# Writing the output in three column groups of 256 instead of two halves of 384, with fewer loads between the stores

## The chip, the core and the metric

The kernel runs on one core of a Trainium2 chip. The metric is the device time of one execution in microseconds (us). TensorE is called PE here, VectorE DVE, ScalarE ACT, GpSimd POOL, and SyncE, which in this kernel only issues transfers (DMAs), SP.

## The reference

An attention with a sigmoid in place of the softmax feeds a soft mixture of experts: 8 batches of 448 tokens (3584 in all), 12 heads of 64 (768 columns), 8 experts with 4 slots each (32 slots), hidden width 1024, all in 32-bit floats.

```python
scores = scale * (q @ k.T) - log(S); x = sigmoid(scores) @ v         # x: 3584 x 768
logits = x @ phi                                                     # 3584 x 32
d = softmax of logits over the tokens;  slot_input = d.T @ x         # 32 x 768
h = relu(slot_input[e] @ w1[e]);  slot_out[e] = h @ w2[e]            # w1: 8 x 768 x 1024, w2: 8 x 1024 x 768
c = softmax of logits over the slots;  out = c @ slot_out            # out: 3584 x 768
```

w1 and w2 hold 25 MB each, and the output 11 MB.

## The kernel before

**Stages.** The first stage is the attention with the logits and the slot inputs; it ends near 298 us, and the change does not touch it. Then come two stages: w1 (`w1_part` and `h_part`, one expert after another), and w2 with the output, from the loop at L600 to the end.

**Weights.** They are cut on the host into 128 units of 128 x 768 floats, 384 KB each: units 0 to 63 are w1, 64 to 127 are w2. In the kernel before a w2 unit holds, for one half of the output columns (`HALF` = 384), two of the 64 pieces of 128 rows that the 8 experts have together (`NFC` = 8 per expert). Units go in order into a ring of 68 tiles (`ring_tile`: 49 called wa, 19 called wb). `load_unit` issues the next one on SP. In the attention 49 are issued, 19 after it, and the others by `load_more` in the loops over w1 and over the first half of w2, as tiles come free; `load_more` stops `N_LATE` = 16 units before the end. SP issues in program order, and a transfer that waits holds up all that come after it.

**w2.** `w2_step` does half an expert: four matmuls whose stationary operand is 128 x 32 (hT), each in its own 32 rows of the PSUM tile `po`, with the columns of the group as moving operand. So 16 steps make one half of the columns. `gather` copies `po` to SBUF on ACT, `sum_groups` adds the four row groups up with one matmul by `rep`, and DVE copies the result to `st`.

**Output.** `out_batch` does one batch of 448 tokens for one half of the columns: four matmuls (128, 128, 96 and 96 tokens), then two evictions into ring tiles, one by ACT (2 x 128 tokens) and one by DVE (2 x 96 tokens), and two stores that are put in a list. Each store writes pieces of one row's columns: 256 and 192 pieces per batch. `store(n)` issues the first n in the list on SP.

**Order.** The first half's outputs are written while the second half's steps run: in step i = 3 + b stands `out_batch` of batch b. In the first `N_MIX` = 4 of these, SP gets two stores and then four of the late units. `warm(3)` puts three small matmuls on PE that only keep it busy. After the last step SP gets what is left in the list (batches 4 to 7 of the first half), then the second half's eight batches follow.

Of the kernel before, what the change touches and what calls it, by code (L numbers as in the profile page):

```python
# [9 lines left out]
F32 = mybir.dt.float32  # L10
# [6 lines left out]
B, H, S, D = 8, 12, 448, 64  # L17
DM, NSLOT, E, SPE, F = 768, 32, 8, 4, 1024
P = 128
# [3 lines left out]
NQ = NPR // 2  # L23
NKC = DM // P
NFC = F // P
HALF = DM // 2
UNIT = 768
N_A = 49
N_B = 19
N_LATE = 16  # L30
N_MIX = 4
NATT = 5
QW = 2 * S
NP = B * NPR
# [6 lines left out]
TOK = (128, 128, 96, 96)  # L41
# [6 lines left out]
def soft_moe_attention(ctx: ExitStack, tc: tile.TileContext, qk, v, phi, w1, w2, cst, out):  # L48
    nc = tc.nc
# [7 lines left out]
    ident = csb[:, 0:128]  # L57
    rep = csb[:, 128:256]
# [4 lines left out]
    lt_all = cpool.tile([P, B, P], F32, name="lt_all")  # L63
# [6 lines left out]
    nc.gpsimd.memset(lt_all, NEG)  # L70

    units = [("w1", e, 2 * uu + y, kh) for e in range(E) for uu in range(2) for kh in range(2) for y in range(2)]
    units += [("w2", hf, e, g, y) for hf in range(2) for e in range(E) for g in range(2) for y in range(2)]
    state = {"next": 0, "ring": 0, "wpb": None}
    utile = {}

    def ring_tile(dt=F32):
        n = state["ring"]
        state["ring"] = n + 1
        n %= N_A + N_B  # L80
        if n < N_A:
            return wpa.tile([P, UNIT], dt, name=f"wa{n}")
        return state["wpb"].tile([P, UNIT], dt, name=f"wb{n - N_A}")

    def load_unit():
        n = state["next"]
        if n >= len(units):
            return
        state["next"] = n + 1
        u = units[n]  # L90
        t = ring_tile()[:]
        nc.sync.dma_start(t, w1[u[1:]] if u[0] == "w1" else w2[u[1:]])
        utile[u] = t
# [22 lines left out]
    with ExitStack() as actx:  # L116
# [216 lines left out]
        def last_job(b, lg):  # L333
# [15 lines left out]
            nc.scalar.activation(pe, lg, AF.Exp, bias=cw[:, 0:1])  # L349
            nc.scalar.activation(cw[:, 1:2], mz[:, 0:1], AF.Exp, bias=cw[:, 0:1])  # L350
            warm(2)
            nc.tensor.matmul(pa[0:1, 0, 0:P], m1[:, 1:2], ident, start=True, stop=True)
            warm(2)
            widen(b, pe)
            mrow = small.tile([1, 1, NSLOT], F32, name="mrow")
# [3 lines left out]
            for j in range(4):  # L359
                nc.tensor.matmul(pa[32 * j:32 * j + 32, 1, 0:1], mrow[:, 0, :], csb[0:1, 0:1], start=True, stop=True)  # L360
            warm(1)
            sl = slot_mm(b, (2, 3))
            nc.vector.tensor_tensor(out=cw[:, 2:3], in0=m1[:, 1:2], in1=pa[:, 1, 0:1], op=ALU.subtract)
# [123 lines left out]
    sb2 = ctx.enter_context(tc.tile_pool(name="sb2", bufs=1, reuse_waits="tile"))  # L487
    hT = []
# [11 lines left out]
    ps_o = ctx.enter_context(tc.tile_pool(name="ps_o", bufs=2, space=PSUM, reuse_waits="tile"))  # L500

    def px_tile():
        return ps_x.tile([P, 2, 512], F32, name="px")

    def load_more():
        if state["next"] < len(units) - N_LATE:
            load_unit()

    for _ in range(N_B):
# [2 lines left out]
    def w1_part(e):  # L512
        ph = px_tile()
        for uu in range(2):
            for k2 in range(NKC // 2):
                for j in range(4):
                    kh, kc = divmod(2 * k2 + j % 2, 3)
                    nc.tensor.matmul(  # L518
                        ph[32 * j:32 * j + 32, uu, 0:256], sT[:, 3 * kh + kc, :],
                        utile[("w1", e, 2 * uu + j // 2, kh)][:, kc * 256:(kc + 1) * 256],  # L520
                        start=(k2 == 0), stop=(k2 == NKC // 2 - 1))
                if k2 > 0:
                    load_more()
                    load_more()
            if e == 0 and uu == 0:
                finish(ps_x)
        return ph
# [26 lines left out]
            combine_d(B - 1, sb2.tile([P, P], F32, name="tmp")[:])  # L554
    h_part(*prev)

    def out_batch(hf, b, st):
        pf = [px_tile() for _ in range(2)]
        for j in range(4):
            r = slice(32 * j, 32 * j + 32)  # L560
            nc.tensor.matmul(  # L561
                pf[j // 2][0:TOK[j], j % 2, 0:HALF], lt_all[r, b, 0:TOK[j]], st[r, :], start=True, stop=True)
        for g in range(2):
            n = TOK[2 * g]
            ov = ring_tile()[0:n, :].rearrange("p (j c) -> p j c", j=2)
            (nc.scalar.copy if g == 0 else nc.vector.tensor_copy)(ov, pf[g][0:n, :, 0:HALF])  # L566
            r0 = b * S + TOF[2 * g]
            stores.append((out[r0:r0 + 2 * n, hf * HALF:(hf + 1) * HALF].rearrange("(j p) c -> p j c", p=n), ov))

    stores = deque()  # L570

    def store(n):
        for _ in range(min(n, len(stores))):
            nc.sync.dma_start(*stores.popleft())

    def warm(n):
        for _ in range(n):
            nc.tensor.matmul(wt[:, 0:P], ident, ident, start=True, stop=True)

    def w2_step(po, hf, e, g):  # L580
        for fl in range(4):
            ut = utile[("w2", hf, e, g, fl // 2)][:, fl % 2 * HALF:(fl % 2 + 1) * HALF]
            nc.tensor.matmul(  # L583
                po[32 * fl:32 * fl + 32, 0:HALF], hT[e][:, 4 * g + fl, :], ut,
                start=(e == 0 and g == 0), stop=(e == E - 1 and g == 1))

    def gather(po):
        so = sb2.tile([P, HALF], F32, name="tmp")
        nc.scalar.copy(so[:], po[:, 0:HALF])
        return so  # L590

    def sum_groups(so):
        pr = px_tile()[:, 0, :]
        nc.tensor.matmul(pr[:, 0:HALF], rep, so[:], start=True, stop=True)
        st = sb2.tile([P, HALF], F32, name="st", bufs=2)
        nc.vector.tensor_copy(st[:], pr[:, 0:HALF])  # L596
        return st

    po = ps_o.tile([P, 512], F32, name="po")
    for e in range(E):  # L600
        for g in range(2):
            w2_step(po, 0, e, g)
            load_more()
            load_more()
    so = gather(po)
    po = ps_o.tile([P, 512], F32, name="po")
    wt = ps_o.tile([P, 512], F32, name="po")
    for i in range(2 * E):
        w2_step(po, 1, *divmod(i, 2))
        if i == 1:  # L610
            st = sum_groups(so)
        if 3 <= i < 3 + B:
            out_batch(0, i - 3, st)
            if i < 3 + N_MIX:
                store(2)
                for _ in range(N_LATE // N_MIX):
                    load_unit()
        if 2 + B <= i < 2 * E - 2:
            warm(3)
    so = gather(po)  # L620
    store(len(stores))
    st = sum_groups(so)
    for b in range(B):
        out_batch(1, b, st)
        store(2)


# [33 lines left out]
```

## Time and profile before

| what | value |
|---|---|
| time, median of 3 runs | 397.97 us (396.63 to 399.82) |
| time of the profiled execution | 401.23 us |
| its span on the core | 399.5 us |
| mean granted PE clock | 0.98 |
| busy: PE, DVE, ACT | 93%, 57%, 47% |
| read from HBM, written to it | 85.43 MB, 11.47 MB |
| transfers of weights | 128 of 384 KB |
| transfers of output | 16 of 384 KB, 16 of 288 KB |

Times inside the execution are counted from the span's start. Two things lie beside the span: the 1.7 us between it and the execution's time, and the difference between this execution and the median of the runs, which is 3.3 us lower. A busy PE is not a PE at its limit, since the ends of its matmuls are modelled; and a DMA share of 1.0 or a little more means that all 16 engines move data all the time.

### The profile page before, as it was taken

Reading aid. Unit: us, or ns where it says so; the run is one execution under the profiler, and the core shown is the slowest. Engines: PE = TensorE matmul, PEld = TensorE weight load, DVE = VectorE, ACT = ScalarE, POOL = GpSimd, SP = SyncE. Lnnn points to the kernel's source line nnn. Section 1 sums busy time; section 2 is a strip of 40 time slices with the busy share of each in tenths; the row PEclk is TensorE's granted clock in tenths of the full one; section 3 lists DMA queues with packets and bytes.
Section 4 is the critical chain, followed back from the end, with each engine's and each line's share of the span. In section 5 each row is a group of like instructions: output and inputs, shape, how many; then the busy total and the mean of one; then the engine's idle time right before and its main releaser. Section 6 shows DMA issues by size and latency. Waiting matters only on the chain.

```text
span 399.5 us, 9562 instructions
## 1 busy us (share of the span) xinstructions
PE 371.3 (93%) x4000; PEld 195.1 (49%) x4000; DVE 228.7 (57%) x531; ACT 186.1 (47%) x244; POOL 3.4 (1%) x13
## 2 busy tenths in 40 slices
PE   8999999999999999899999999999989989978740
PEld 6555455555545555365545556555465543223210
DVE  3566668668777766765677777677532420330340
ACT  5655666662566656265625666564530110220330
POOL 1000000000000000000000000000010000000000
PEclk9999999999999999989999999999999999999985
DMA  7556567645655755475546656632899999999996
GB/s 237 197 189 232 180 235 257 222 150 161 225 199 192 276 199 178 140 250 178 180 120 251 220 175 239 235 126 71 304 344 334 405 400 400 400 410 409 355 288 205
DMA packets 41851, 97.52 MB, mean 244 GB/s; under 512 B 4304, under 2 KB 16208, under 8 KB 41808
## 3 DMA queue, kind: packets, MB, share of 16 engines
q1 hardware_dynamic: 41808, 96.91, 69.1%
q8 instruction: 31, 0.51, 0.5%
q14 instruction: 12, 0.10, 0.1%
HBM read 85.43 MB, written 11.47 MB: 243 GB/s over the span
## 4 chain that ended last, share of the span: by engine, by line
PE 78%; DMA 12%; DVE 3%; issue 2%; SPq 1%; ACT 0%; ACTq 0%
PE b L186 25%; PE b L168 21%; PE b L195 6%; PE px L518 5%; PE b L307 4%; PE po L583 4%; PE b L179 4%; DMA wb<-in_w_dram 4%; DMA zd<-t 3%; PE b L215 3%; PE px L561 2%; DMA dr<-zd 2%; DMA wa<-in_w_dram 2%; DMA out_dram<-wa 1%; PE px L535 1%
## 5 line engine op out<-in xcount | busy, mean ns | idle before, releaser
L158 ACT ACTIVATE att<-b,nbias 128x896 f32<-128x896 f32 x144 | 132.1, 1020 | 1.3 <-PE b L168 1.1
L186 PE MATMUL b<-att,v 128*64 128x448 f32 x576 | 115.3, 545 | 0.1
L168 PE MATMUL b<-qs,ks 64*128 64x448 f32 x864 | 96.3, 373 | 0.7 <-issue 0.5
L168 PEld LDWEIGHTS b<-qs,ks 64*128 64x128 f32 x864 | 80.2, 188 | 24.8 <-PE b L195 14.8
L186 PEld LDWEIGHTS b<-att,v 128*64 128x64 f32 x576 | 38.5, 137 | 62.6 <-issue 47.4
L158 ACT ACTIVATE attm<-b,nbias 128x896 f32<-128x896 f32 x24 | 24.2, 1010 | 71.6 <-PE b L179 71.6
L147 DVE CAST qs<-qkt 128x448 fp32r<-128x448 f32 x48 | 18.8, 392 | 51.5 <-DMA qkt<-in_qk_dram 47.4
L149 DVE TENSOR_TENSOR qs<-qkt,qs 128x448 fp32r<-128x448 f32 x48 | 30.0, 626 | 1.6
L204 DVE COPY xT<-b 128x896 f32<-128x896 f32 x23 | 25.1, 1090 | 8.6 <-PE b L195 8.5
L149 DVE TENSOR_TENSOR ks<-qkt,ks 128x384 fp32r<-128x384 f32 x48 | 26.8, 558 | 1.6
L210 DVE STREAM_TRANSPOSE y<-xT 128x448 f32<-128x448 f32 x48 | 27.3, 618 | 0.4
L179 PE MATMUL b<-qkt 64*64 64x448 f32 x192 | 22.9, 538 | 2.2 <-issue 2.2
L195 PE MATMUL b<-attm,v 64*64 64x448 f32 x192 | 23.6, 562 | 0.0
L307 PE MATMUL b<-y,dr 32*32 32x192 f32 x896 | 20.0, 332 | 0.8 <-DMA dr<-zd 0.5
L566 DVE COPY wa<-px 96x768 f32<-96x768 f32 x13 | 12.2, 952 | 13.5 <-PE px L561 12.7
L518 PE MATMUL px<-wa,sT 128*32 128x256 f32 x294 | 17.8, 381 | 0.9 <-DVE sT L378 0.9
L566 ACT COPY wa<-px 128x768 f32<-128x768 f32 x13 | 10.3, 799 | 17.9 <-PE px L561 15.2
L561 PE MATMUL px<-st,lt_all 32*128 32x384 f32 (+1 forms) x128 | 16.7, 525 | 1.5 <-DVE st L596 0.7
L215 PEld LDWEIGHTS b<-xT,phit 128*32 128x32 f32 x384 | 9.1, 109 | 17.0 <-issue 11.3
L147 DVE CAST ks<-qkt 128x384 fp32r<-128x384 f32 x47 | 16.6, 353 | 0.0
L215 PE MATMUL b<-xT,phit 128*32 128x96 f32 (+1 forms) x384 | 16.0, 266 | 0.2
L307 PEld LDWEIGHTS b<-y,dr 32*32 32x32 f32 x896 | 12.8, 103 | 6.5 <-DMA dr<-zd 2.3
(132 smaller groups left out, 223.4 us busy)
## 6 DMA issues: line engine op xcount, KB each, us to landing
wa<-in_w_dram SPq DMA_DIRECT2D x96, 384.0 KB, 7.7
qkt<-in_qk_dram SPq DMA_DIRECT2D x48, 448.0 KB, 5.0
wb<-in_w_dram SPq DMA_DIRECT2D x32, 384.0 KB, 7.1
v<-in_v_dram SPq DMA_DIRECT2D x24, 448.0 KB, 3.3
out_dram<-wa SPq DMA_DIRECT2D x13, 384.0 KB, 5.8
out_dram<-wa SPq DMA_DIRECT2D x13, 288.0 KB, 5.6
dr<-zd SPq DMA_DIRECT2D x28, 64.0 KB, 2.0
out_dram<-wb SPq DMA_DIRECT2D x3, 384.0 KB, 7.3
```

What stands on the lines that cost most here:

```text
L147: copy(dst[:, 0, :], src)
L149: nc.vector.tensor_tensor(out=dst[:, 1, :], in0=src, in1=dst[:, 0, :].bitcast(F32), op=ALU.subtract)
L158: nc.scalar.activation(att[:], sc[:, :, 0:S], AF.Sigmoid, bias=nbias, scale=QSCALE)
L168: nc.tensor.matmul(sc[:, h, 0:S], ks[r, z, c * P:(c + 1) * P], qs[r, y, :], start=(z + y == 0), stop=(z == 1))
L179: nc.tensor.matmul(sc[r, h, 0:S], t[d, S + NQK:QW], t[d, 0:S], start=True, stop=True)
L186: nc.tensor.matmul(avs["p", p][r, 0:S], vs[n][:, i * (NFULL + 1) + c, r], atts[p, c][:, h, :], start=(start and c == 0), stop=(stop and c ...
L195: nc.tensor.matmul(avs["p", 2 * n + i][d, 0:S], vt[r, NFULL, d], att[r, h, :], start=start, stop=stop)
L204: nc.vector.tensor_copy(xTs[n][:], avs[n][:, :, 0:S])
L210: nc.vector.transpose(ys[b][:, hp, :], xTs["p", p])
L215: nc.tensor.matmul(lp[32 * j:32 * j + 32, 0:TOK[j]], phi_sb[:, p % NPR, :], xTs["p", p][:, TOF[j]:TOF[j] + TOK[j]], start=(first and m == ...
L307: nc.tensor.matmul(sl[a // 2][32 * j:32 * j + 32, a % 2, 0:NPR * BLK], drs[b][32 * a:32 * a + 32, j, c * BLK:(c + 1) * BLK], y[32 * a:32 * ...
L518: nc.tensor.matmul(ph[32 * j:32 * j + 32, uu, 0:256], sT[:, 3 * kh + kc, :], utile[("w1", e, 2 * uu + j // 2, kh)][:, kc * 256:(kc + 1) * ...
```

## The change

Columns are written in three groups of 256 (`CG`). The host cuts w2 anew: a unit now holds three pieces of 128 x 256, so a group takes 21 1/3 units, and a step 1 1/3. There are 24 batches of output in place of 16, each with pieces of 1024 B in place of 1536 B (stores of 256 KB and 192 KB). The groups are called 0, 1 and 2 here. All but 18 units are issued ahead. Between the stores of group 0 stand eight of those 18, one after each batch; between the stores of group 1 stand ten, two after each of its first five batches. `warm` is gone.

```diff
-HALF = DM // 2
+NCG = 3
+CG = DM // NCG
-N_LATE = 16
-N_MIX = 4
+LATE = ((1,) * B, (2,) * 5)
...
-    units += [("w2", hf, e, g, y) for hf in range(2) for e in range(E) for g in range(2) for y in range(2)]
+    units += [("w2", i) for i in range(NCG * E * NFC // 3)]
...
     def load_more():
-        if state["next"] < len(units) - N_LATE:
+        if state["next"] < len(units) - sum(LATE[0] + LATE[1]):
...
-    def warm(n):
-        for _ in range(n):
-            nc.tensor.matmul(wt[:, 0:P], ident, ident, start=True, stop=True)
...
-    def w2_step(po, hf, e, g):
+    def w2_step(po, cg, e, g):
         for fl in range(4):
-            ut = utile[("w2", hf, e, g, fl // 2)][:, fl % 2 * HALF:(fl % 2 + 1) * HALF]
+            u, y = divmod((cg * E + e) * NFC + 4 * g + fl, 3)
             nc.tensor.matmul(
-                po[32 * fl:32 * fl + 32, 0:HALF], hT[e][:, 4 * g + fl, :], ut,
+                po[32 * fl:32 * fl + 32, 0:CG], hT[e][:, 4 * g + fl, :], utile["w2", u][:, y * CG:(y + 1) * CG],
                 start=(e == 0 and g == 0), stop=(e == E - 1 and g == 1))
...
+    for cg in range(NCG):
+        po = ps_o.tile([P, 512], F32, name="po")
+        for i in range(2 * E):
+            w2_step(po, cg, *divmod(i, 2))
+            if cg == 0:
+                load_more()
+                load_more()
+                continue
+            if i == 1:
+                st = sum_groups(so)
+            if 3 <= i < 3 + B:
+                b = i - 3
+                out_batch(cg - 1, b, st)
+                if b < len(LATE[cg - 1]):
+                    store(2)
+                    for _ in range(LATE[cg - 1][b]):
+                        load_unit()
+        so = gather(po)
     store(len(stores))
     st = sum_groups(so)
     for b in range(B):
-        out_batch(1, b, st)
+        out_batch(NCG - 1, b, st)
         store(2)
```

On SP, before, at the end of the units issued ahead (wa and wb are ring tiles, filled from the weights by L92, or written to the output by L574):

```order
L92 DMA wa_4031<-in_w_dram 128x768
L92 DMA wa_4033<-in_w_dram 128x768
L574 DMA out_dram<-wa_4240 128x2x384
L574 DMA out_dram<-wa_4242 96x2x384
L92 DMA wa_4246<-in_w_dram 128x768
L92 DMA wa_4248<-in_w_dram 128x768
L92 DMA wa_4250<-in_w_dram 128x768
L92 DMA wb_4252<-in_w_dram 128x768
L574 DMA out_dram<-wb_4264 128x2x384
L574 DMA out_dram<-wb_4266 96x2x384
```

And now, at the same place:

```order
L92 DMA wa_4025<-in_w_dram 128x768
L574 DMA out_dram<-wa_4235 128x2x256
L574 DMA out_dram<-wa_4237 96x2x256
L92 DMA wa_4241<-in_w_dram 128x768
L574 DMA out_dram<-wa_4253 128x2x256
L574 DMA out_dram<-wa_4255 96x2x256
L92 DMA wa_4259<-in_w_dram 128x768
L574 DMA out_dram<-wa_4271 128x2x256
L574 DMA out_dram<-wb_4273 96x2x256
L92 DMA wb_4277<-in_w_dram 128x768
```

The first store has moved ahead of two units (those that were in wa_4031 and wa_4033), and one batch of stores stands ahead of every late unit here, where it was one batch ahead of four.

On SP, before, around the last unit (the rows end with the last group's first batch):

```order
L92 DMA wb_4324<-in_w_dram 128x768
L574 DMA out_dram<-wa_4336 128x2x384
L574 DMA out_dram<-wa_4338 96x2x384
L574 DMA out_dram<-wa_4350 128x2x384
L574 DMA out_dram<-wa_4352 96x2x384
L574 DMA out_dram<-wa_4364 128x2x384
L574 DMA out_dram<-wa_4366 96x2x384
L574 DMA out_dram<-wa_4378 128x2x384
L574 DMA out_dram<-wa_4380 96x2x384
L574 DMA out_dram<-wa_4434 128x2x384
L574 DMA out_dram<-wa_4436 96x2x384
```

And now:

```order
L92 DMA wa_4504<-in_w_dram 128x768
L92 DMA wa_4506<-in_w_dram 128x768
L574 DMA out_dram<-wa_4518 128x2x256
L574 DMA out_dram<-wa_4520 96x2x256
L574 DMA out_dram<-wa_4532 128x2x256
L574 DMA out_dram<-wa_4534 96x2x256
L574 DMA out_dram<-wa_4546 128x2x256
L574 DMA out_dram<-wa_4548 96x2x256
L574 DMA out_dram<-wa_4588 128x2x256
L574 DMA out_dram<-wa_4590 96x2x256
```

Between the last unit and the last group's first store stood four batches; now there are three smaller ones.

On PE, before, the end of the w2 steps (L583, in the PSUM tile po), the `warm` matmuls (L578), the sum (L594) and the first output of the last group (L561):

```order
L583 MATMUL po<-wb_4294,h_3698 32x384 x2
L583 MATMUL po<-wb_4296,h_3698 32x384 x2
L578 MATMUL po<-csb 128x128 x3
L583 MATMUL po<-wb_4298,h_3698 32x384 x2
L583 MATMUL po<-wb_4300,h_3698 32x384 x2
L578 MATMUL po<-csb 128x128 x3
L583 MATMUL po<-wb_4318,h_3699 32x384 x2
L583 MATMUL po<-wb_4320,h_3699 32x384 x2
L583 MATMUL po<-wb_4322,h_3699 32x384 x2
L583 MATMUL po<-wb_4324,h_3699 32x384 x2
L594 MATMUL px<-tmp,csb 128x384
L561 MATMUL px<-st,lt_all 128x384 x2
```

And now, from the last batch of group 1 on (L579 are the steps, L590 is the sum):

```order
L561 MATMUL px<-st,lt_all 96x256 x2
L579 MATMUL po<-wa_4446,h_3697 32x256 x2
L579 MATMUL po<-wa_4464,h_3697 32x256 x2
L579 MATMUL po<-wa_4464,h_3698 32x256
L579 MATMUL po<-wa_4466,h_3698 32x256 x3
L579 MATMUL po<-wa_4484,h_3698 32x256 x3
L579 MATMUL po<-wa_4486,h_3698 32x256
L579 MATMUL po<-wa_4486,h_3699 32x256 x2
L579 MATMUL po<-wa_4504,h_3699 32x256 x3
L579 MATMUL po<-wa_4506,h_3699 32x256 x3
L590 MATMUL px<-tmp,csb 128x256
L561 MATMUL px<-st,lt_all 128x256 x2
```

The matmuls between these steps are gone, and a unit serves three matmuls where it served two.

More of the change, by code (lines that the diff above doesn't have):

```diff
@@ L555, in soft_moe_attention, with out_batch @@
     h_part(*prev)
-    def out_batch(hf, b, st):
+    def out_batch(cg, b, st):
         pf = [px_tile() for _ in range(2)]
@@ L561, in out_batch @@
             nc.tensor.matmul(
-                pf[j // 2][0:TOK[j], j % 2, 0:HALF], lt_all[r, b, 0:TOK[j]], st[r, :], start=True, stop=True)
+                pf[j // 2][0:TOK[j], j % 2, 0:CG], lt_all[r, b, 0:TOK[j]], st[r, :], start=True, stop=True)
         for g in range(2):
             n = TOK[2 * g]
-            ov = ring_tile()[0:n, :].rearrange("p (j c) -> p j c", j=2)
-            (nc.scalar.copy if g == 0 else nc.vector.tensor_copy)(ov, pf[g][0:n, :, 0:HALF])
+            ov = ring_tile()[0:n, 0:2 * CG].rearrange("p (j c) -> p j c", j=2)
+            (nc.scalar.copy if g == 0 else nc.vector.tensor_copy)(ov, pf[g][0:n, :, 0:CG])
             r0 = b * S + TOF[2 * g]
-            stores.append((out[r0:r0 + 2 * n, hf * HALF:(hf + 1) * HALF].rearrange("(j p) c -> p j c", p=n), ov))
+            stores.append((out[r0:r0 + 2 * n, cg * CG:(cg + 1) * CG].rearrange("(j p) c -> p j c", p=n), ov))
     stores = deque()
@@ L574, in store @@
             nc.sync.dma_start(*stores.popleft())
-    def warm(n):
-        for _ in range(n):
-            nc.tensor.matmul(wt[:, 0:P], ident, ident, start=True, stop=True)
-    def w2_step(po, hf, e, g):
+    def w2_step(po, cg, e, g):
         for fl in range(4):
-            ut = utile[("w2", hf, e, g, fl // 2)][:, fl % 2 * HALF:(fl % 2 + 1) * HALF]
+            u, y = divmod((cg * E + e) * NFC + 4 * g + fl, 3)
             nc.tensor.matmul(
-                po[32 * fl:32 * fl + 32, 0:HALF], hT[e][:, 4 * g + fl, :], ut,
+                po[32 * fl:32 * fl + 32, 0:CG], hT[e][:, 4 * g + fl, :], utile["w2", u][:, y * CG:(y + 1) * CG],
                 start=(e == 0 and g == 0), stop=(e == E - 1 and g == 1))
     def gather(po):
-        so = sb2.tile([P, HALF], F32, name="tmp")
-        nc.scalar.copy(so[:], po[:, 0:HALF])
+        so = sb2.tile([P, CG], F32, name="tmp")
+        nc.scalar.copy(so[:], po[:, 0:CG])
         return so
@@ L593, in sum_groups @@
         pr = px_tile()[:, 0, :]
-        nc.tensor.matmul(pr[:, 0:HALF], rep, so[:], start=True, stop=True)
-        st = sb2.tile([P, HALF], F32, name="st", bufs=2)
-        nc.vector.tensor_copy(st[:], pr[:, 0:HALF])
-        return st
[L599 to L620, printed above, removed]
+        nc.tensor.matmul(pr[:, 0:CG], rep, so[:], start=True, stop=True)
+        st = sb2.tile([P, CG], F32, name="st", bufs=2)
+        nc.vector.tensor_copy(st[:], pr[:, 0:CG])
+        return st
+    for cg in range(NCG):
[16 more added lines that the diff above has]
+        so = gather(po)
     store(len(stores))
@@ L642 @@
     w1 = inputs["moe_w1"].reshape(E, 2, 3, P, 4, 256).transpose(0, 4, 1, 3, 2, 5).reshape(E, 4, 2, P, UNIT)
-    w2 = inputs["moe_w2"].reshape(E, 2, 2, 2, P, 2, HALF).transpose(5, 0, 1, 3, 4, 2, 6).reshape(2, E, 2, 2, P, UNIT)
+    w2 = inputs["moe_w2"].reshape(E, 2, 2, 2, P, NCG, CG).transpose(5, 0, 1, 3, 2, 4, 6).reshape(-1, 3, P, CG)
+    w2 = w2.transpose(0, 2, 1, 3).reshape(-1, P, UNIT)
     cst = np.zeros((P, CW), np.float32)
```

## The prediction

> **What bounds the kernel now.** I read the page first, then a table by stretches, then the chain that ended last, and at the end the rows of single operations. The page's 40 slices (10 us each) give the first answer.
>
> ```profile
> span 399.5 us, 9562 instructions
> DMA  7556567645655755475546656632899999999996
> GB/s 237 197 189 232 180 235 257 222 150 161 225 199 192 276 199 178 140 250 178 180 120 251 220 175 239 235 126 71 304 344 334 405 400 400 400 410 409 355 288 205
> ```
>
> PE has 93% of the span on the page, but that is an average over stages. In the last eleven slices the transfer engines are full, and in the last three they are still full while the GB/s fall from 409 to 355, 288 and 205. The table by stretches shows what else works there.
>
> ```profile
> core 0: us, PE busy (x) PEld busy (x) DVE busy (x) ACT busy (x) POOL busy (x), PEclk, DMA share, GB/s
> 330.00:344.00 14.00, 14.00 (x150) 4.91 (x142) 1.43 (x2) 1.28 (x2) 0.00 (x0) 1.00 1.03 401
> 344.00:371.00 27.00, 23.21 (x166) 7.98 (x164) 6.76 (x8) 5.59 (x7) 0.00 (x0) 1.00 1.04 407
> 371.00:375.00 4.00, 2.62 (x16) 0.93 (x16) 0.56 (x1) 0.48 (x1) 0.00 (x0) 1.00 1.07 397
> 378.00:396.00 18.00, 6.20 (x40) 2.28 (x40) 5.58 (x7) 4.12 (x6) 0.00 (x0) 0.74 0.90 280
> 396.00:399.50 3.50, 0.00 (x0) 0.00 (x0) 0.00 (x0) 0.00 (x0) 0.00 (x0) 0.50 0.24 69
> ```
>
> Loads alone (330 to 344), loads mixed with stores (344 to 371) and the first stores alone (371 to 375) all run at 397 to 407 GB/s. Then something changes: from 378 to 396 only stores are left, the engines show 0.90 busy, and they move 280 GB/s. No compute engine is busy for more than 6.2 of these 18 us. So **the end is a queue of transfers**: it starts full and ends in a slow stretch of stores. The chain names the same.
>
> ```profile
> 356.53 7.32 DMA wb<-in_w_dram
> ...
> 363.92 7.35 DMA wb<-in_w_dram
> ...
> 371.33 5.76 DMA out_dram<-wa
> ...
> 384.60 0.95 DVE wa L566
> ```
>
> The last unit lands at 363.92 + 7.35 = 371.3. The last eviction ends at 385.6, 13.9 us before the span does, so the stores alone set the end.
>
> **What the change does to the queue, up to the last weights.** The bytes stay the same; pieces of output shrink from 1536 B to 1024 B, and stores and loads change order. The price of a piece comes from the two stretches that hold one kind alone.
>
> ```profile
> DMA packets 2048, 5.61 MB, mean 401 GB/s; under 512 B 227, under 2 KB 227, under 8 KB 2047
> DMA packets 834, 1.20 MB, mean 398 GB/s; under 512 B 56, under 2 KB 834, under 8 KB 834
> ```
>
> The first row is 330 to 344: 2047 - 227 = 1820 pieces of 3072 B (the 227 are 4-byte signals), 14.0 us x 16 engines x 1.03 / 1820 = 127 ns each. The second is 371.6 to 374.6 with a share of 1.066: 834 - 56 = 778 pieces of 1536 B, 3.0 x 16 x 1.066 / 778 = 66 ns. A line through both gives 46 ns for 1024 B, which this trace has in no stretch of its own. A batch is 448 pieces, before and after: 448 x 66 / (16 x 1.066) = **1.73 us before and 1.20 after** (448 x 46). The bounds are 1.15 (the same time per byte) and 1.73 (the same time per piece); I take 1.20, as the two rows lie on one line.
>
> Ahead of the last unit in SP's order stood 112 + 16 units and 4 batches; now there are 110 + 18 units and 8 + 5 = 13 batches. The engines are full all along, so the last unit lands 13 x 1.20 - 4 x 1.73 = 8.7 us later, at **380.0** (bounds 379.3 and 386.9).
>
> This needs the queue to stay full, and the change adds waits to it: every late unit now stands on SP behind two stores that wait for an eviction, and group 2's steps wait for these units.
>
> ```profile
> 300.49 41.20 SPq L92 DMA_DIRECT2D wa<-in_w_dram  x44
> 343.90 0.90 SPq L574 DMA_DIRECT2D out_dram<-wa  x2
> 376.13 0.38 SPq L574 DMA_DIRECT2D out_dram<-wa  x1
> ```
>
> SP is through with the last unit ahead at 341.7, waits for the first eviction until 343.9, and the stretch from 344 on still moves 407 GB/s: the 7 us of transfers that are under way cover such a wait. In the change it gets to the first store two units (2 x 0.98 us, 384 KB at 401 GB/s) earlier, at 339.7. When is that store ready?
>
> ```profile
> 327.43 11.75 PE po L583 x144
> 308.90 2.80 PE L518 MATMUL px<-wa,sT 128*32 128x256 f32 x48
> 337.96 0.48 ACT L589 COPY tmp<-po 128x384 f32<-128x384 f32 x1 [9.70 <-PE po L583]
> 339.11 0.91 PE L594 MATMUL px<-tmp,csb 128*128 128x384 f32 x2
> 340.06 0.56 DVE L596 COPY st<-px 128x384 f32<-128x384 f32 x1 [12.13 <-PE px L594]
> 342.11 0.92 PE L561 MATMUL px<-st,lt_all 32*128 32x384 f32 x8
> 343.07 0.80 ACT L566 COPY wa<-px 128x768 f32<-128x768 f32 x1 [4.63 <-PE px L561]
> ```
>
> A matmul in the program is two instructions in the trace. The w2 steps start at 327.4, and 256 columns into 32 rows cost 2.80 / 48 = 58 ns (L518, the same shape). Group 0's 128 instructions end at 334.9, four steps of group 1 (32) take 1.9, and the sum, its copy, one batch and its eviction at their old prices 0.91 + 0.56 + 0.92 + 0.80 = 3.2: 340.0 at the latest, 339 with two thirds of these prices. After that PE needs 0.5 us per step and at most 0.9 per batch, against 1.20 + 0.98 = 2.2 us of transfers per batch and unit. Of the later stores, batch b of group 1 needs the units up to 111 + 1.33 b, which stand six or more units and five batches ahead of it in SP's order, over 11 us of transfers. So I cost these waits at nothing; the cover is the transfers under way, and where it is gone, a late eviction costs its whole lateness. ACT and DVE get 24 evictions each in place of 16, of two thirds the width, beside the queue; POOL does nothing here.
>
> **The end, from the last weights on.** Before, the last group's first store is issued at 376.13, 4.9 us after the last landing (the last step, `gather`, sum, copy, one batch, one eviction). Two thirds of that would be 3.3, nothing saved 4.9; I take 3.7. Behind the last unit stand three batches of group 1, 3 x 1.20 = 3.6 us at the full rate and 4.9 at 280 GB/s, so the queue runs dry for one to three us before group 2 comes; before, four batches of 1.73 covered that.
>
> From 376.13 to the end are 23.3 us. Eight batches of 672 KB at 280 GB/s are 8 x 2.46 = 19.7; the other 3.6 are the way into the queue and out of it. Now eight batches of 448 KB take 13.1 at the same 280 GB/s (1.64 each), bounded by 9.6 (1.20 each, the slow stretch does not come) and 19.7 (2.46, the same time per piece). I take 1.64, since it is the rate measured in the stretch itself. Nothing in the trace says whether it counts bytes or pieces.
>
> **PE's clock.** `warm` goes, and group 2's last five steps hold 8 x 58 = 0.46 us of work each, while their units land 1 1/3 x 0.98 + 0.67 x 1.20 = 2.1 us apart: 22% busy. The trace has a stretch like it.
>
> ```profile
> 168.10:171.50 3.40, 1.24 (x14) 1.00 0.45 141
> 171.50:175.00 3.50, 3.50 (x23) 0.51 0.63 168
> L578 PE MATMUL po<-csb 128*128 128x128 f32 x24 | 3.7, 292 | 0.0
> ```
>
> After 3.4 us in which PE was 36% busy, the granted clock was 0.51 for the next 3.5 us (PEclk is the column after the parenthesis). The 3.7 us of `warm` (L578) lie in front of the last units. Without them I expect half the clock when the last unit lands. It doubles the PE parts of the 3.7 us, some 0.46 + 0.61 + 0.61 = 1.7, to 5.4. The Trainium skill ("TensorE: Matmul & The Clock Gate", Part 1: The HAM clock gate) has the clock fall after an idle window of about 3.4 us. Read strictly, PE's short pieces of work would keep the clock up, and the 1.7 us would not be paid; the row above, 36% busy and still halved, speaks for paying them. If PE runs at half the clock in the last group, a batch takes it 1.2 us, less than 1.64.
>
> **The sum.** 380.0 + 5.4 + 3.6 + 13.1 = **402.1**, against 399.5: 2.6 us more. The weights come 8.7 later, and the end behind them shrinks from 28.2 to 22.1. The profiled execution took 401.23 us, and the median of the runs is 397.97; I put the difference on the median: **400.6 us**.
>
> **Rivals.**
>
> *The clock stays up.* Then 1.7 us fall away: 400.4, median 398.9. For it: while PE still has batches to do, it is about half busy. Against it: the row at 168.
>
> *The slow stretch does not come.* With three batches in place of four ahead, a dry moment and less to write in one piece, the stores could keep 1.20 us. For it: the row at 371 to 375, stores alone at 397 GB/s. Against it: all of the last group before ran at 280. Half the clock gives 380.0 + 5.4 + 3.6 + 9.6 = 398.6 and the full clock 396.9: medians 397.1 and 395.4, and 394 with every lower bound. Even so the gain is small, because three full groups of bytes still pass the same queue.
>
> *The pieces are the price (slower).* Where stores meet a limit per piece and not per byte, the last eight batches take 2.46 each again: 380.0 + 5.4 + 3.6 + 19.7 = 408.7, median 407.2. A milder form lies in the mixed stretch: between 344 and 371 about 30% of the bytes were stores (4 batches, 16 units), in group 0's stretch 54% will be (448 of 832 KB); at 280 GB/s there, 13 x 0.44 = 5.7 us come on top of 402.1, median 406.3. It decides from 50 ns per 1024-byte piece in the mix on: 13 batches x 448 x 4 ns / 17.06 are 1.4 us on top of the forecast, and that is slower by 1%. For it: the slow stretch has 90% share and low GB/s, so its pieces are stretched. Against it: 66 and 127 ns lie on a line with a small constant. The Trainium skill ("DMA: Bandwidth & Descriptors", section Bandwidth) says to batch transfers to at least 1 MiB and puts 64 KB at 32% of the peak, which speaks against smaller stores; an estimate of half the peak, 218 GB/s, would give 2.1 us per batch in the tail and 405.8 in all. The trace does not bear it out where transfers queue: stores of 384 and 288 KB ran at 398 GB/s.
>
> *It doesn't do what it says.* Evictions come late and SP's waits empty the queue. Each 1 us of lateness in eight batches would be 8 us. PE's 1.4 us per batch against 2.2 speak against it.
>
> **How the numbers follow.** The forecast has 0.35 (its own range, from both bounds of the 3.7 and of 1.20, is 399 to 402.5 on the median), the clock that stays up 0.20, full-rate stores 0.22, the price per piece 0.20, late evictions 0.03. The range goes from 394.5, the low end of the full-rate case, to 407.5. A measurement tells about 1% here: under 394.0 or over 402.0. Faster by that is only the luckiest half of the full-rate case, 0.12. Slower is the price per piece, late evictions and a third of the forecast, 0.35. Within 1%: 0.53.
>
> **What would show it.** The last unit should land at 380 in the new trace, and 344 to 376 should stay at 390 to 407 GB/s. The last group's first store should be issued near 385.4 with PEclk near 0.5 just before it. The stores after it should move 280 GB/s at 0.9 share; 380 would be the second rival, 190 the third. I am wrong at the root if the share falls below 1 before the last unit lands.

## The result and the profile after

| | before | changed |
|---|---|---|
| time, median of 17 runs each | 398.42 us (395.23 to 403.24) | 401.77 us (398.65 to 404.60) |
| time of the profiled execution, its span | 401.23 us, 399.5 us | 401.65 us, 399.9 us |
| mean granted PE clock | 0.98 | 0.96 |

The ratio of the times is 1.0093 with an interval of 1.0066 to 1.0119: the change costs 3.35 us on the medians, 2.6 to 4.7 us by the interval, and the prediction had 2.6. The ratios leave out executions over 1.5% above the fastest of their kernel (3 of the 17 of before here), and here and below a ratio can differ by up to 0.4% from the quotient of the medians, which count all. The two spans differ by only 0.4 us, because the profiled execution of before lies 2.8 us over its median and the one of the changed kernel lies at its own. That has to be kept in mind when the two traces are laid side by side; it comes back further down.

The page of the changed kernel, lines for the span and the 40 slices:

```profile
span 399.9 us, 9962 instructions
PEclk9999999999999999999999999999989999989855
DMA  6556567655665765476456557443899999999957
GB/s 219 177 185 234 211 204 262 202 196 156 217 218 183 243 220 182 149 258 218 146 183 234 181 190 279 163 146 97 286 337 376 402 400 401 396 396 399 398 180 235
```

The rate now stays at 396 to 402 until 380, one slice longer than before, and then falls in one step to 180: the slice from 380 to 390 shows DMA 5, where before it had 9. PEclk drops to 8 in the slice before it and to 5 in this one. The changed kernel's table by stretches (columns as in the table of before) resolves the hole.

```profile
344.00:370.00 26.00, 20.77 (x224) 7.99 (x218) 7.29 (x11) 6.24 (x11) 0.00 (x0) 0.93 1.06 397
370.00:380.00 10.00, 6.13 (x49) 1.43 (x48) 0.69 (x1) 0.61 (x2) 0.00 (x0) 0.80 1.06 397
380.00:382.00 2.00, 1.22 (x2) 0.50 (x2) 0.34 (x1) 0.35 (x1) 0.00 (x0) 0.50 0.60 210
382.00:384.00 2.00, 1.86 (x12) 1.19 (x12) 0.62 (x2) 0.59 (x1) 0.00 (x0) 0.50 0.00 0
384.00:388.00 4.00, 4.00 (x28) 2.15 (x26) 2.19 (x4) 1.76 (x3) 0.00 (x0) 0.50 0.75 223
388.00:396.00 8.00, 4.95 (x30) 2.39 (x28) 2.77 (x5) 2.35 (x4) 0.00 (x0) 0.50 0.94 284
```

Up to 380 the engines are full (share 1.06) at 397 GB/s, with the small stores in the mix. From 382 to 384 they move nothing. Counted by the share, 0.40 x 2 + 1.00 x 2 + 0.25 x 4 = 3.8 us of transfer time are lost between 380 and 388. Before has no such place: from 376 to 396, in steps of 4 us, its shares lie between 0.85 and 0.95. After the hole the stores go on at 284 GB/s with 0.94 share, as they did before at 280 with 0.90. The chain that ended last shows who works during the hole (start, duration; its pieces under 0.1 us are left out):

```profile
371.68 6.12 DMA wa<-in_w_dram
377.84 2.05 PE po L579 x12
379.98 0.38 ACT tmp L585
380.40 1.24 PE px L590 x2
381.66 0.44 DVE st L592
382.14 10.84 PE px L561 x62
```

It is the way from the last weights to the last group's first output: the weights, the last matmuls of `w2_step` (L579), the copy of `gather` (L585), the sum (L590), its copy (L592), and then `out_batch`. In before's chain a store, not a load, stood at this place. The rows in order of time give the moments:

```profile
379.98 0.37 ACT L585 COPY tmp<-po 128x256 f32<-128x256 f32 x1 [8.58 <-PE po L579]
382.14 10.81 PE L561 MATMUL px<-st,lt_all 32*128 32x256 f32 x64 [0.52 <-DVE st L592]
383.41 0.59 ACT L566 COPY wa<-px 128x512 f32<-128x512 f32 x1 [3.06 <-PE px L561]
384.02 0.38 SPq L574 DMA_DIRECT2D out_dram<-wa  x1
```

`gather` starts at 379.98, where before it stood at 372.25, and the first store of the last group is issued at 384.02, where before it was 376.13: both 7.7 to 7.9 us later. From that store to the end of the span are 15.9 us, 23.3 before.

### The profile page after: what moved, and what is told of

Its sections match the earlier page's. It is cut to its first block, busy times and chain, and to the rows that moved or that the text cites. A ratio compares the mean times of both kernels' runs of the same rounds, so it can differ in the third digit from the quotient of the medians.

```text
span 399.9 us, 9962 instructions
## 1 busy us (share of the span) xinstructions
PE 376.6 (94%) x4170; PEld 200.0 (50%) x4170; DVE 230.0 (58%) x540; ACT 187.3 (47%) x253; POOL 3.4 (1%) x13
## 4 chain that ended last, share of the span: by engine, by line
PE 79%; DMA 14%; DVE 2%; issue 1%; SPq 1%; ACT 1%; ACTq 0%
PE b L186 25%; PE b L168 20%; DMA wa<-in_w_dram 6%; PE px L518 6%; PE b L195 6%; PE b L179 4%; PE b L307 4%; PE px L561 3%; PE po L579 3%; DMA zd<-t 3%; PE b L215 3%; DMA out_dram<-wb 3%; DMA dr<-zd 2%; PE px L535 1%; PE b L402 1%
## 5 line engine op out<-in xcount | busy, mean ns | idle before, releaser
L168 PE MATMUL b<-qs,ks 64*128 64x448 f32 x864 | 95.1, 369 | 0.7 <-issue 0.7
L168 PEld LDWEIGHTS b<-qs,ks 64*128 64x128 f32 x864 | 78.6, 184 | 25.9 <-PE b L195 16.2
L561 PE MATMUL px<-st,lt_all 32*128 32x256 f32 (+1 forms) x192 | 23.8, 525 | 0.5 <-DVE st L592 0.5
L566 DVE COPY wa<-px 96x512 f32<-96x512 f32 x17 | 11.7, 687 | 21.6 <-PE px L561 21.6
L179 PE MATMUL b<-qkt 64*64 64x448 f32 x192 | 23.8, 554 | 0.0
L566 ACT COPY wa<-px 128x512 f32<-128x512 f32 x18 | 10.6, 586 | 26.0 <-PE px L561 22.5
L518 PE MATMUL px<-wa,sT 128*32 128x256 f32 x294 | 19.1, 401 | 0.9 <-DVE sT L378 0.9
L561 PEld LDWEIGHTS px<-st,lt_all 32*128 32x128 f32 (+1 forms) x192 | 11.5, 213 | 12.5 <-issue 5.4
L579 PE MATMUL po<-wa,h 128*32 128x256 f32 x144 | 12.5, 411 | 4.5 <-DMA wa<-in_w_dram 4.5
```

The costliest lines, as they stand in the source:

```text
L168: nc.tensor.matmul(sc[:, h, 0:S], ks[r, z, c * P:(c + 1) * P], qs[r, y, :], start=(z + y == 0), stop=(z == 1))
L179: nc.tensor.matmul(sc[r, h, 0:S], t[d, S + NQK:QW], t[d, 0:S], start=True, stop=True)
L518: nc.tensor.matmul(ph[32 * j:32 * j + 32, uu, 0:256], sT[:, 3 * kh + kc, :], utile[("w1", e, 2 * uu + j // 2, kh)][:, kc * 256:(kc + 1) * ...
L561: nc.tensor.matmul(pf[j // 2][0:TOK[j], j % 2, 0:CG], lt_all[r, b, 0:TOK[j]], st[r, :], start=True, stop=True)
L579: nc.tensor.matmul(po[32 * fl:32 * fl + 32, 0:CG], hT[e][:, 4 * g + fl, :], utile["w2", u][:, y * CG:(y + 1) * CG], start=(e == 0 and g == ...
```

## The experiments

Each is a small edit of one of the two kernels. Ratios are to the kernel before, run on the same chip beside it (its medians were 398.56, 398.96 and 399.14 us). In the edits, `...` stands for lines left out. The theory is that the hole costs the time, because too few stores stand behind the last weights; the rivals are the halved clock and the smaller pieces.

### The clock kept up

The changed kernel, with small matmuls that only keep PE busy after the last steps of the last group:

```diff
...
+            if cg == NCG - 1 and 2 + B <= i < 2 * E - 1:
+                warm(wt, 4)
```

> The changed kernel with warm back: four small matmuls after each of group 2's steps 10 to 14. Theory A (the loss is the dry moment of the queue after the last weights, made longer by PE at half the clock): the granted clock is 1.0 when the last unit lands, the last group's first store is issued about 1.5 us earlier than in the changed kernel (384.0 minus 1.5, shifts of the whole trace aside), and the last unit lands at the same place; 1.5 to 2.5 us less, a ratio to the kernel before near 1.004. Theory B (the smaller pieces are what costs, order and clock do not matter): the ratio stays at 1.009.

Measured: 402.48 us, ratio 1.0101 (1.0066 to 1.0136). Stretches of this kernel:

```profile
374.00:384.00 10.00, 9.98 (x88) 6.09 (x84) 0.69 (x1) 0.58 (x1) 0.00 (x0) 1.00 1.06 396
384.00:388.00 4.00, 2.68 (x32) 1.51 (x24) 1.11 (x2) 1.45 (x3) 0.00 (x0) 1.00 0.34 117
388.00:396.00 8.00, 5.16 (x50) 2.40 (x44) 4.63 (x7) 3.51 (x6) 0.00 (x0) 1.00 0.95 287
```

The granted clock is 1.00 in these stretches, and the hole is still there: 0.66 x 4 = 2.6 us by the share (this whole execution runs a few us late). So the clock is not what makes the hole. From `gather` to the first store this kernel takes 3.0 us, the changed one 4.0. The clock shortens this part by 1 us, and an interval of 1.4 us to either side cannot show it. The edit also takes something back, since `warm` (L597) stands in the way of the last step (L579) on PE:

```profile
382.57 1.16 PE L597 MATMUL po<-csb 128*128 128x128 f32 x8
383.66 0.64 PE L579 MATMUL po<-wa,h 128*32 128x256 f32 x8
```

The last unit has landed at 382.9, and its step starts 0.7 us later, when `warm` is through.

### More stores behind the last weights

The changed kernel, with the late units moved ahead in SP's order: two after each batch of group 0, and the last two after group 1's first batch. Nine batches stand ahead of the last unit, and seven behind it (three in the changed kernel).

```diff
-LATE = ((1,) * B, (2,) * 5)
+LATE = ((2,) * B, (2,))
```

> The changed kernel with the 18 late units issued two after each batch of group 0 and two after the first batch of group 1, so that 9 batches stand ahead of the last unit in place of 13, and 7 behind it in place of 3. Theory A: the last unit lands 4 x 1.2 = 4.8 us earlier, the 7 batches behind it (8 us) cover the way to the last group's first store, and the share no longer falls between the two; the 3 to 4 us of dry time go, but some 4 more batches fall into the slow stretch of stores alone, 4 x 0.44 = 1.8 us: 1.5 to 3 us less, ratio 1.002 to 1.006. Theory B: 1.009.

Measured: 398.11 us, ratio 1.0014 (0.9978 to 1.0051). By the ratios 3.1 us are gone, where I expected 1.5 to 3, with all the small pieces kept and the clock halved:

```profile
344.00:370.00 26.00, 21.15 (x234) 8.01 (x234) 7.37 (x12) 6.22 (x11) 0.00 (x0) 1.00 1.05 398
370.00:376.00 6.00, 3.73 (x24) 0.74 (x24) 0.00 (x0) 0.07 (x1) 0.00 (x0) 0.60 1.06 394
376.00:380.00 4.00, 3.13 (x15) 1.69 (x15) 1.00 (x2) 0.88 (x2) 0.00 (x0) 0.50 1.07 366
380.00:392.00 12.00, 8.90 (x54) 4.53 (x52) 4.92 (x8) 4.10 (x7) 0.00 (x0) 0.50 0.95 291
```

In these stretches the share does not fall below 0.95, in spite of PEclk 0.50; there is no hole. This is the run that tells the theories apart: the order alone gives the loss back.

### Both

The same `LATE`, and `warm` as in the first experiment.

> Both edits together: warm back in group 2's steps, and the late units two after each batch of group 0. Theory A: with the queue covered, the first store is not what the queue waits for, and the clock adds nothing: the same as with the units moved alone, within 0.3%, ratio 1.002 to 1.005. Rival C (PE at half the clock needs 1.35 us per batch in the last group and so holds up the stores there): faster than the units moved alone by over 1 us, ratio at or below 1.000.

Measured: 398.44 us, ratio 0.9991 (0.9956 to 1.0025). With the way covered, the clock at the last landing adds nothing that can be told: this run and the one before it lie within each other's intervals. Rival C's ratio is met, but the run does not test it, since the clock falls here too once the last group's stores have begun:

```profile
380.00:384.00 4.00, 4.00 (x30) 2.20 (x28) 2.06 (x3) 1.76 (x3) 0.00 (x0) 0.50 0.96 295
```

### The kernel before, without `warm`

```diff
...
-        if 2 + B <= i < 2 * E - 2:
-            warm(3)
```

> The kernel before without warm, nothing else. The clock may fall to half before the last unit lands. Theory A: four batches of 1.73 us (6.9) stand behind the last unit, and the first store comes 4.9 + 1.7 = 6.6 us after it at half the clock, so the loss stays covered: ratio 1.000 to 1.003. Rival C (PE's pace at half the clock holds up the last group's stores): over 1 us more, ratio 1.003 to 1.008.

Measured: 397.68 us, ratio 1.0019 (0.9979 to 1.0059). Stretches:

```profile
344.00:370.00 26.00, 19.06 (x130) 4.59 (x128) 6.58 (x7) 5.33 (x7) 0.00 (x0) 1.00 1.03 393
370.00:374.00 4.00, 2.62 (x14) 0.66 (x14) 0.56 (x1) 0.48 (x1) 0.00 (x0) 1.00 1.07 396
378.00:392.00 14.00, 5.74 (x40) 1.94 (x32) 5.03 (x6) 3.99 (x5) 0.00 (x0) 0.82 0.97 307
```

In the kernel before the clock stays at 1.00 without `warm`, up to the last group, and the time is the same. (In one of the twelve executions the mean clock is 0.956, in the others 0.973 to 0.985, so it need not stay up every time.) In the changed kernel it falls without `warm` (0.50) and stays up with it (the first experiment). Why only there stays open. The last row is a second reading of before's tail: 307 GB/s, where the profiled execution of before has 280. The work there is the same.

### The hole in the kernel before, without small pieces

Halves as before, but two late units after each of the eight batches of the first half, so that no store stands behind the last unit:

```diff
-N_MIX = 4
+N_MIX = 8
```

> The kernel before (two halves, pieces of 1536 B) with the 16 late units issued two after each of the first half's eight batches in place of four after each of four, so that all of the first half's stores stand ahead of the last unit and none behind it. Theory A (order: the weights come later and the queue runs dry behind them): the last unit lands 4 x 1.73 = 6.9 us later, near 378, the queue is dry for 5 to 6 us after it, 4 batches leave the stretch of stores alone (some 3 us back): 2.5 to 5 us more, ratio 1.006 to 1.012, with no small pieces in it. Theory B (the smaller pieces cost): ratio 1.000.

Measured: 406.28 us, ratio 1.0214 (1.0171 to 1.0257). Stretches:

```profile
374.00:378.00 4.00, 1.80 (x10) 0.41 (x12) 0.00 (x0) 0.00 (x0) 0.00 (x0) 1.00 0.82 318
378.00:382.00 4.00, 2.65 (x14) 0.65 (x16) 0.56 (x1) 0.48 (x1) 0.00 (x0) 1.00 0.01 3
382.00:386.00 4.00, 3.39 (x28) 1.59 (x29) 2.39 (x3) 2.30 (x3) 0.00 (x0) 1.00 0.38 121
386.00:402.00 16.00, 5.77 (x40) 1.94 (x32) 5.06 (x6) 4.00 (x5) 0.00 (x0) 0.76 0.96 304
```

The order alone, with pieces of 1536 B and the clock at 1.00, makes a hole of 0.18 x 4 + 0.99 x 4 + 0.62 x 4 = 7.2 us by the share, and the medians differ by 7.3 us (6.8 to 10.3 by the ratio's interval). In the changed kernel the hole is 3.8 us and the medians differ by 3.35. Hole and loss agree in both, as far as intervals of 2 to 3.5 us in width can tell. My expectation was too low: I had the queue dry for 5 to 6 us, and I had counted on getting back 3 us for four batches that leave the slow stretch, but in before these batches had run at 397 GB/s (its row from 371 to 375), so there was nothing to get back.

### Fewer stores behind, at full clock

Five batches behind the last unit in place of seven, with `warm`:

```diff
-LATE = ((2,) * B, (2,))
+LATE = ((2,) * 5 + (1,) * 3, (2, 2, 1))
```

> The changed kernel with warm back and the late units two after each of group 0's first five batches, one after each of its last three, then two, two and one in group 1: 11 batches stand ahead of the last unit and 5 behind it (13 and 3 in the changed kernel, 9 and 7 with the units moved alone). Theory A: 5 x 1.2 = 6.0 us cover the 4.5 us from the last landing to the first store and about 1 us until its pieces move, so the queue stays filled, and two batches fewer than with 7 behind lie in the slow stretch: 0 to 1 us less than that, ratio 0.995 to 1.000. Rival: where the cover does not suffice, the share falls below 0.9 before the last group, ratio 1.000 to 1.004.

Measured: 399.0 us, ratio 1.0012 (0.9972 to 1.0051). Stretches:

```profile
374.00:378.00 4.00, 3.37 (x30) 1.83 (x29) 0.05 (x1) 0.37 (x1) 0.00 (x0) 1.00 1.01 343
378.00:382.00 4.00, 3.02 (x34) 1.85 (x36) 2.35 (x4) 1.66 (x3) 0.00 (x0) 1.00 0.87 271
382.00:390.00 8.00, 3.82 (x34) 1.76 (x32) 3.35 (x5) 2.92 (x5) 0.00 (x0) 0.86 0.96 293
```

There is a dip to 0.87 and no hole, and no gain over seven behind that can be told. The dip and the ratio are those of the rival, but the interval reaches to theory A as well. With the clock kept up, five batches are enough within this interval; three are not (the first experiment).

### What limits the stores at the end

With the hole explained, the slow stretch (280 to 309 GB/s at a share near 1) stays. First: is it SP, which alone issues the stores? The kernel of the third experiment ("Both"), and then the kernel before, with the last group's ACT evictions stored from ACT's own queue:

```diff
-        store(2)
+        nc.scalar.dma_start(*stores.popleft())
+        store(1)
```

> The changed kernel with warm back, the late units two after each batch of group 0, and in the last group the store of each ACT eviction issued on ACT's queue, the other one on SP's. Theory W (stores alone settle at 280 GB/s because the memory takes no more from this core): the tail keeps 270 to 300 GB/s, the time is that of the same kernel with one queue within 0.3%, ratio 0.996 to 1.002. Theory I (one queue's issue, which stands blocked for 1 to 2 us at a time in that stretch, starves the engines): the last 8 batches run at 380 GB/s, 8 x 0.44 = 3.5 us less, ratio near 0.990.

> The kernel before, with the store of each ACT eviction of the second half issued on ACT's queue. Theory W: tail at 280 GB/s as before, ratio 0.998 to 1.003. Theory I: the last 8 batches of 1.73 us in place of 2.46, 5.8 us less, ratio near 0.985.

Measured: 397.97 us, ratio 0.9984 (0.9954 to 1.0014), and 399.4 us, ratio 1.0022 (0.9993 to 1.0051). The row of the first kernel, then that of the second:

```profile
382.00:390.00 8.00, 3.70 (x24) 2.12 (x20) 2.63 (x4) 1.85 (x4) 0.00 (x0) 0.50 1.00 292
```

```profile
378.00:394.00 16.00, 6.60 (x44) 2.37 (x40) 5.84 (x7) 4.79 (x6) 0.00 (x0) 0.82 1.00 303
```

The share is 1.00 and the rate stays at 292 and 303: one issuing queue is not the limit. More stores are also under way at once, as the times from issue to landing show (count, size, median us; the kernel before, then the same with two queues, both from 378 to 396):

```profile
out_dram<-wa SPq DMA_DIRECT2D x7, 384.0 KB, 5.4
out_dram<-wa ACTq DMA_DIRECT2D x6, 384.0 KB, 8.6
out_dram<-wa SPq DMA_DIRECT2D x7, 288.0 KB, 8.5
```

A store of 384 KB takes 8.6 us in place of 5.4, and the rate does not rise.

Second: is there room beside the stores? The kernel before, with one load of 384 KB that nobody needs behind each batch of the second half:

```diff
         store(2)
+        nc.sync.dma_start(ring_tile()[:], w1[b, 0, 0])
```

> The kernel before, with one unneeded load of a 384 KB weight unit into a free ring tile issued behind each of the second half's eight batches of stores: 3.1 MB more to move. Theory W: the engines have room for 400 GB/s and only the stores are held to 280, so about 19.7 us x 120 GB/s = 2.4 MB of the loads cost nothing: the tail moves 350 to 400 GB/s, and the time grows by 1 to 3 us, ratio 1.003 to 1.008. Theory E (the engines themselves are full in the slow stretch, at 0.9 share): each load adds its 0.98 us or more, 8 us in all, ratio 1.018 to 1.025.

Measured: 406.12 us, ratio 1.0210 (1.0159 to 1.0262).

```profile
382.00:402.00 20.00, 1.72 (x10) 0.46 (x8) 1.91 (x2) 1.60 (x2) 0.00 (x0) 0.57 1.00 336
```

Eight loads, 3.1 MB, cost 7.2 us on the medians, or 0.9 each, and 8.4 us by the ratio, or 1.05 each. That is the price of a unit in the full queue before, 0.98 us. So loads on SP's queue find no room in this stretch; loads on another queue were not tried.

Third: is it the size or the place of the pieces? The kernel before, with the second half's stores as whole rows, 3072 B per piece; half of the rows never get their second half, and the others' first half is overwritten, so that the bytes are the same:

```diff
+            if hf:
+                stores.append((out[r0:r0 + n, :], ov.rearrange("p j c -> p (j c)")))
+            else:
+                stores.append((out[r0:r0 + 2 * n, hf * HALF:(hf + 1) * HALF].rearrange("(j p) c -> p j c", p=n), ov))
```

> The kernel before, with the second half's stores written as 128 or 96 whole rows of 3072 B in place of twice as many half rows of 1536 B (the same bytes in as many stores; half of the rows are left out and the first half's columns of the others overwritten, so the output is not the reference's). Theory R (half rows at a pitch of 3072 B are what slows stores alone): the tail runs at 380 to 400 GB/s, 5 to 6 us less, ratio 0.985 to 0.988. Theory W (stores alone are slow by bytes, whatever the piece): 270 to 300 GB/s, ratio 0.998 to 1.003.

Measured: 398.3 us, ratio 1.000 (0.996 to 1.004).

```profile
378.00:394.00 16.00, 4.44 (x30) 1.64 (x28) 3.94 (x5) 3.20 (x5) 0.00 (x0) 0.78 0.86 286
```

The packets of the same stretch:

```profile
DMA packets 1705, 4.58 MB, mean 286 GB/s; under 512 B 219, under 2 KB 219, under 8 KB 1703
```

286 GB/s with pieces of 3072 B, beside 284 with 1024 B and 280 to 309 with 1536 B. Over these sizes the stretch is slow by the byte, whatever the piece.

Fourth: is it that the stores come one by one? In two single runs the second half's stores were to be held back until all eight batches were done. The first only wrote them behind the batches in the program:

```diff
         out_batch(1, b, st)
-        store(2)
+    store(len(stores))
```

> The kernel before, with all 16 stores of the second half issued after its last eviction and not between: the queue is dry for some 9 us, then 16 stores are issued with nothing to wait for. Theory S (stores alone run at 400 GB/s for about 5 us and only then settle at 280): the first 4 us move 380 to 400 GB/s, later ones 280 to 300. Theory Q (they run at full speed as long as the queue is deep): 380 to 400 GB/s to the end. Theory W (stores alone are slow from the first one, unless loads ran just before): 280 to 300 from the start.

Measured: 395.81 us in one run. This edit changes nothing: SP's order is the same, each store waits for its own eviction only, and the first is issued at 372.76. It serves as a third reading of before's tail:

```profile
374.00:390.00 16.00, 6.57 (x44) 2.27 (x40) 6.22 (x7) 4.76 (x6) 0.00 (x0) 0.80 0.98 309
```

The second also turned the list round (`stores.reverse()`), so that SP waits for the last eviction first, and none of the 16 stores then has to wait for one.

> The kernel before, with the second half's 16 stores issued in reverse order behind all eight batches, so that SP waits for the last eviction first and then has 16 stores whose data lie ready. The queue is dry for some 8 us before them. Theory S (stores alone run at 400 GB/s for about 5 us and then settle at 280): the first 4 us of the last group move 380 to 400 GB/s, later ones 280 to 300. Theory Q (full speed as long as the queue is deep): 380 to 400 GB/s to the end, 14 us for the eight batches. Theory W (slow from the first store on, unless loads ran just before): 280 to 300 from the start, 19 to 20 us for the eight batches.

Measured: 408.6 us in one run, beside 399.27 for the kernel before.

```profile
370.00:375.00 5.00, 3.48 (x16) 0.73 (x14) 0.49 (x1) 0.48 (x1) 0.00 (x0) 1.00 1.06 395
380.00:385.00 5.00, 4.74 (x32) 1.69 (x30) 3.63 (x4) 3.57 (x5) 0.00 (x0) 1.00 0.01 2
389.00:401.00 12.00, 0.00 (x0) 0.00 (x0) 0.00 (x0) 0.00 (x0) 0.00 (x0) 0.52 1.00 322
```

With the data ready and nothing else running, the stores move 322 GB/s, with no faster part at the start (330 from 389 to 393). That is neither theory S nor theory Q, and a little over the range of theory W. The queue gets no deeper by this edit: SP issues the 16 stores one by one from 386.4 to 400.7, with five under way at a time, as in before. So depth is tested by the two queues above and not here. The first row shows once more that the stores directly behind the loads (the last one landed at 372.1) still run at 395.

**What stays open.** Stores alone settle near 280 to 320 GB/s, and neither the one issuing queue, nor the number of stores under way, nor the piece, nor the waits for evictions is the reason. What it is, and why the first 4 us or so behind the loads are still fast, I cannot say.

## Why the prediction held, and where it was off

**The end is a full queue, and the change puts more ahead of the last weights.** Right. The queue stayed full and at 397 GB/s up to the last weights, as the first two stretches of the changed kernel show, so the price per piece of 46 ns in the mix and "these waits at nothing" both held. (One reading of mine was loose: the last of the 40 slices was not full, its digit is 6, as the stores run out there.) The last unit landed at 378.8 by its own record in the trace (371.3 before), where I had 380.0. Of the 1.2 us between, 0.8 were there when the late units began: the last unit issued ahead went out at 338.6, against 339.4 for the same place in before's trace. `gather` moved by 7.7 us, or 8.5 from that common start, against 8.7 in the sum.

**Three batches don't cover the way.** Right in kind, too small in size: I wrote one to three us, and 3.8 us are missing by the share. The way (5.3 us) and the three batches (3.6) are as I had them, 1.7 us apart; the other 2 us lie at the two ends of the hole, which I left out.

```profile
381.00:382.00 1.00, 0.62 (x2) 0.00 (x0) 0.34 (x1) 0.00 (x0) 0.00 (x0) 0.50 0.39 136
384.00:385.00 1.00, 1.00 (x10) 0.76 (x10) 0.15 (x1) 0.59 (x1) 0.00 (x0) 0.50 0.06 19
385.00:386.00 1.00, 1.00 (x9) 0.30 (x4) 0.69 (x1) 0.52 (x1) 0.00 (x0) 0.50 1.03 314
```

The engines run out by 382, where 378.8 + 3.6 would be 382.4, and the first store, issued at 384.02, moves its bytes only from about 385 on. In the kernel with halves and nothing behind the last unit, the engines are at 0.31 from 377 to 378 already, and the unit's landing is recorded at 378.7. The sum did not need the length of the hole, since it counts from the recorded landing to the issue and has 3.6 us for the way in and out. The experiment with seven batches behind shows that this is the cause (1.0014 in place of 1.0093), and the one with halves shows that it does not need small pieces (1.0214).

**The clock.** It fell to 0.50 as expected, and the way from the last landing to the first store took 5.3 us (I had 5.4). At full clock, in the first experiment, it took 4.5, where I had 3.7; but 0.7 of the 4.5 are the wait for `warm`. An estimate without that wait is 3.8 us, so that about 1.5 us belong to the clock, where the sum had 1.7. That `warm` kept the clock up before was wrong: without it the clock was 1.00 all the same.

**The tail at the same bytes per second.** Right: 284 GB/s, where the price per piece would have given 190. The packets from 388 to 396 are 2222 pieces (2378 less the 156 small ones), or 278 per us, where 280 GB/s before were 280 / 1.536 = 182 per us.

```profile
DMA packets 2378, 2.28 MB, mean 284 GB/s; under 512 B 156, under 2 KB 2378, under 8 KB 2378
```

From the first store to the end the changed kernel takes 15.9 us, and the sum had 13.1 + 3.6 = 16.7.

**The base.** Here luck comes in. On the two traces the change costs 0.4 us and not 2.6: the sum ends at 402.1, and the changed kernel's span is 399.9. Of the 2.2 us between, 1.2 lie in the landing and most of the rest in the tail. The medians differ by 3.35 all the same, because the execution that I started from was a long one. Its tail ran at 280 GB/s, against 307 and 309 in two other executions of the same stores, which take 21.6 and 21.2 us from the first store to the end, not 23.3. Against those the changed kernel's tail saves 5.5 us, not the 7.4 that the two traces show. Landing 7.5 later, 0.4 for the way, 5.5 saved: 2.4 us, and 3.2 with the 0.8 of the common start, beside the 3.35 measured. That is worked out across executions and was not measured in one, and the landing moves too: from the issue at that common place to the last landing the trace of before takes 31.8 us, six others with the same transfers up to there take 32.2 to 33.6, and the changed kernel 40.1. So the 2.6 came near because the sum was too high for the changed kernel by about as much (2.2 us) as the execution that it started from lay over its median (2.8).

**The rivals.** *The clock stays up* and *full-rate stores* are refuted by the rows 0.50 and 284. *The pieces are the price* is refuted by the tail's 284 and by the order experiment, which keeps all small pieces and loses nothing that can be told. The Trainium skill ("DMA: Bandwidth & Descriptors", section Bandwidth) says to batch transfers to at least 1 MiB. This case does not bear that out in a queue that is full: the stores of 256 and 192 KB moved 397 GB/s in the mix, and 284 to 291 alone, where the larger ones had 280 to 309. *Late evictions* didn't come. SP's queue in the changed kernel, in order of time:

```profile
339.58 1.34 SPq L574 DMA_DIRECT2D out_dram<-wa  x2
...
371.68 1.29 SPq L92 DMA_DIRECT2D wa<-in_w_dram  x2
```

The first store was issued at SP's turn (I had 339.7), and the share stayed at 1.06 up to the last unit and beyond.

No version tried is faster than the kernel before by more than its interval; the nearest is the one with the order mended, `warm` and two queues (0.9984, 0.9954 to 1.0014).

## What to carry to other kernels

Where the transfers set the end, compare what stands in the queue behind the last load with the time from that load's landing to the first output that depends on it, and add about 2 us, as measured here, for the two ends. What is short of that is a hole in the queue (3.6 against 5.3 + 2, and none against 4.9 + 2, gave holes of 3.8 and 7.2 us), and the time lost was about as long (3.35 and 7.3 us), with small pieces and with larger ones. The four batches of the kernel before, 6.9 us against 4.9 + 2, were just enough. In this kernel the order of the transfers was worth more than their size. A rate that one profiled execution shows, above all at the end, should be read in a second one before a sum rests on it.

## What was not expected of the hardware

Stores directly behind loads run at 395 to 397 GB/s until 3 to 4 us after the last landing, and then stores alone settle at 280 to 320 with the engines shown 0.9 to 1.0 busy. Stores that start into an empty queue have no such fast part (304 GB/s with halves and nothing behind the last unit, 322 with the stores turned round). More stores under way only take longer each (8.6 us in place of 5.4), and a load on the same queue costs its full 0.9 to 1.05 us there, so the stretch has no idle capacity that these runs could use. And the same stores took between 280 and 309 GB/s in different executions of the same order.
